# Converting float64 weights to float32: the rounding of the low word moved from VectorE to ScalarE and GpSimd

## The chip, the cores and the metric

One core of a Trainium2 chip runs the kernel. The metric is device time in microseconds of one execution, the median of several runs. VectorE, ScalarE, GpSimd, TensorE and SyncE are called DVE, ACT, POOL, PE and SP in rows of the profile.

## The reference

The kernel computes sliding-window attention with a linear bias for each head, and passes its output through two gated blocks:

```python
x = attn_out.transpose(0, 2, 1, 3).reshape(2304, 512)   # 4 batches, 8 heads of 64, 576 positions
x = ((x @ moe_w_a) * (x @ moe_w_b)) @ moe_w_out         # 512 -> 1536 -> 512
h = ((x @ moe2_w1) * (x @ moe2_w2)) @ moe2_w3           # 512 -> 1024 -> 1024
out = h @ moe2_w_out                                     # 1024 -> 512
```

q, k and v are float32. The seven weight matrices come as float64 and must be turned into float32 on the chip.

## The kernel before, in words

Each float32 product runs as three passes over a rounded high part and the rest: an operand is split into hi and lo, and lo*hi, hi*lo and hi*hi are summed in PSUM. The second block's w3 @ w_out is formed first and goes through DRAM (w34), so the second block has one product fewer for each token.

The work has three stages. First the attention: 16 units (a batch and two heads) of 5 query blocks each, 80 steps. Beside it a filler gives TensorE the first group's gated products, for tokens that are ready, once that group's six weight tiles are converted. Then the rest of group 0. Then groups 1 to 9: six of the first block, four of the second, each with two 128-column chunks, on tiles of 512 tokens. A chunk's product (`g1`) takes two PSUM accumulators; ScalarE copies one (L526), VectorE multiplies by the other (L528), ScalarE rounds the result to gh (L531), and GpSimd subtracts to get gl (L73). The second product reads gh and gl (L541, L559), and VectorE adds it to an accumulator in SBUF (L548, L566). After the attention eight PSUM tiles go round for all these products.

Weights are converted beside this. A weight tile is [128, 512] float64, loaded by SyncE's queue as pairs of 32-bit words (`raw`, 512 KB: one buffer during the attention, two after it). `convert` returns stages: s0 (ScalarE, L107) takes the absolute value of the high words as float32; s1 is five VectorE instructions: a compare and multiply that makes a mask (L113), the high word's bits shifted and masked (L117), its sign and top exponent bit put in (L120), the exponent alone as a power of two in `ce` (L123), and the low word times that power (L127); s3 (L132, GpSimd) adds the low word's part. Then `split` rounds to hi on ScalarE (L139) and subtracts on GpSimd (L73). The tile `ca` holds the value (two buffers, later three); `ce`, one buffer, holds the low word's part from L123 to L132. The copy of a w3 product on its way to DRAM (L441, L442) uses the same `ce` buffer.

`Stages` emits these stages in turns: a turn gives every part in work its next stage, fetches a load if a raw buffer is free, and starts one more part. A step of the attention pays 0.3 turns in the first batch and 0.6 after it; later each chunk of 512 tokens pays 512/400 turns. There are 76 conversions: 6 for group 0 beside the attention, 24 for w3 @ w_out, the others for groups 1 to 9. The order in which each engine's queue gets its instructions is settled by the framework's scheduler, which takes program order as priority and simulated times for readiness; a tile of a pool with one buffer waits until the last reader of the one before is done.

Of the kernel before, what the change touches and what calls it, by code (L numbers as in the profile page):

```python
# [19 lines left out]

# Float32 products run as three float32r passes: an operand x is the exact sum of
# hi = float32r(x) and lo = x - hi, and x*w = lo*hi' + hi*lo' + hi*hi' to float32's accuracy.
# The second block's w3 @ w_out is formed first: (g @ w3) @ w_out = g @ (w3 @ w_out).
# Weights come as float64: their words are put together as rounded float32 on the chip.

# [4 lines left out]

GROUPS = (6, 4)  # groups of two 128-column chunks of each block's inner features
TA, TN = 256, 512  # tokens of a tile: beside attention, and after it
HALF = 1280  # the token at which the accumulators are cut in two
LAG, NLAG = 8, 2  # steps of attention from the scores to the product with v, and to the norms
AT = (0, 0, 1, 3)  # steps of a unit at which the next one is transposed
V_AT = {2: 1, 6: 2}  # steps at which the second and the third unit's v are loaded
FILL = 0.75  # microseconds of the first group's products in a step of attention
PACE = (0.3, 0.6)  # turns of the weights' conversion in a step: the first batch, the others
TURN = 400  # tokens of a chunk for each turn later
WARM_UNITS, WARM = 3, 2  # L40
# [3 lines left out]
def attention_moe_moe(ctx, tc, q, k, v, w_a, w_b, w_o, w_1, w_2, w_3, w_o2, out):  # L44
# [24 lines left out]
    def f32(ap):  # L69
        return ap.bitcast(F32)  # L70
# [7 lines left out]

    # ---------------------------------------------------------------- weights
    def load_cols(w, c):  # L80
        """128 columns of a [512, .] weight: [128, 4 * 128] with the rows on 4 x 128 partitions."""
        raw = pools["conv"].tile([P, W, 2], I32, name="raw", bufs=pools["raws"])
        nc.sync.dma_start(
            out=raw.rearrange("p (k f) t -> p k (f t)", k=KC),
            in_=w[:, c * P:(c + 1) * P].bitcast(I32).rearrange("(k p) f -> p k f", p=P),
        )
        return raw

    def load_rows(w, r, c):
        """128 rows and 512 columns."""  # L90
        raw = pools["conv"].tile([P, W, 2], I32, name="raw", bufs=pools["raws"])
        nc.sync.dma_start(
            out=raw.rearrange("p f t -> p (f t)"),
            in_=w[r * P:(r + 1) * P, c * W:(c + 1) * W].bitcast(I32),
        )
        return raw

    def convert(raw, hi=None, lo=None, use=()):
        """Float64's two words as float32, to the nearest (0 below float32's exponents), and its
        split: stages, to be emitted one after the other, each when the one before has run."""  # L100
        hw, lw = raw[:, :, 1], raw[:, :, 0].bitcast(U32)
        a = pools["conv"].tile([P, W], F32, name="ca", bufs=pools["cas"])
        ai = a.bitcast(I32)
        es = []

        def s0():
            nc.scalar.activation(a, f32(hw), ACTF.Abs)  # L107

        def s1():
            e = pools["conv"].tile([P, W], F32, name="ce", bufs=1)  # L110
            ei = e.bitcast(I32)
            es.append(e)
            nc.vector.tensor_scalar(  # L113
                out=a, in0=a, scalar1=bits(0x38100000), scalar2=bits(0x3FFFFFF8),
                op0=ALU.is_ge, op1=ALU.mult,
            )
            nc.vector.scalar_tensor_tensor(  # L117
                out=ai, in0=hw, scalar=3, in1=ai, op0=ALU.logical_shift_left, op1=ALU.bitwise_and
            )
            nc.vector.scalar_tensor_tensor(  # L120
                out=ai, in0=hw, scalar=-(1 << 30), in1=ai, op0=ALU.bitwise_and, op1=ALU.bitwise_or
            )
            nc.vector.tensor_scalar(  # L123
                out=ei, in0=ai, scalar1=-(1 << 23), scalar2=None, op0=ALU.bitwise_and
            )

            nc.vector.scalar_tensor_tensor(  # L127
                out=e, in0=lw, scalar=2.0 ** -52, in1=e, op0=ALU.mult, op1=ALU.mult
            )

        def s3():
            nc.gpsimd.tensor_tensor(out=a, in0=a, in1=es[0], op=ALU.add)  # L132

        if hi is None:
            return [s0, s1, s3] + [lambda f=f: f(a) for f in use]
        return [s0, s1, s3, lambda: split(a, hi, lo)]
# [5 lines left out]
    class Stages:  # L142
        """Parts (load, stages of what it loads): a part's stages are emitted in turns one after
        the other, its load ahead of them; its second stage is the last to read the load."""

# [31 lines left out]

    # ---------------------------------------------------------------- attention
    conv_s = ExitStack()
# [15 lines left out]
    def consts():  # L195
# [4 lines left out]
        )  # L200
        # c - p - 128 for key column c of the window and query row p
        rel = raw_2.tile([P, 2 * P], F32, name="rel")
# [11 lines left out]
        )  # L214
        # the bias of each head, as the unscaled scores take it: a power of 2 times up to 8 bits
        for h in range(H):
            nc.gpsimd.tensor_scalar(
                out=relb[:, h, :], in0=rel, scalar1=slope[h] * float(D) ** 0.5, scalar2=None, op0=ALU.mult
            )
        # and for the two heads of a pair below each other  # L220
        for j in range(2):
# [13 lines left out]
    def load_unit(u, which=(0, 1, 2)):  # L235
        b, hp = units[u]
        for x in which:
# [7 lines left out]
            if x:  # L245
# [4 lines left out]
                continue  # L250
            # the last block of q has its two heads on the diagonal, zeros beside them
            for j in range(2):
                o = slice(j * D, (j + 1) * D)
                nc.sync.dma_start(out=t[o, NB - 1, o], in_=s[j, (NB - 1) * P:S, :])

    # q's blocks and k's side by side, as many of them at a time as a bank takes
    cols = [(x, i, (x * NB + i) * P) for x in range(2) for i in range(NB)]
# [3 lines left out]
    def prep(u):  # L261
        """Functions that transpose and split a unit's q, k and v: (tensor engine, others)."""

# [19 lines left out]
        def v_parts():  # L283
            # v's three bfloat16 parts: the upper half of v, of what is left of it, and of what is left then
            vr = v_raws[u % 3]
# [11 lines left out]
    def window(i):  # L297
        """Query rows, keys and key blocks of a query block; the groups of heads that it has side
        by side: the last block's rows are half as many, its two heads fill the partitions."""
        m = P if i < NB - 1 else LAST  # L300
        nb = 1 if i == 0 else 2
        return m, nb * P, nb, 2 if m == P else 1
# [33 lines left out]
    def keep_warm(cnt, x):  # L336
        """Matmuls for the tensor engine's clock alone, which falls when there is little work."""
        ps = mm_tile(W)
# [10 lines left out]
    def probs(u, i):  # L349
# [18 lines left out]
        )  # L368
        # keys, head, part, key block, query
        order = "p (a b c m) -> p a b c m" if nj == 2 else "p (b c a m) -> p a b c m"  # L370
# [36 lines left out]

    # ---------------------------------------------------------------- w3 @ w_out of the second block
    FB = DFF2 // P
# [7 lines left out]
    def w34_parts(pool, halves):  # L417
        """The product's two halves of the contraction, each its own array."""
        NJ = W // P
# [38 lines left out]

    # ---------------------------------------------------------------- gated blocks
    blocks = (dict(a=w_a, b=w_b, o=w_o), dict(a=w_1, b=w_2, o=w34))  # L460
    G1, NG = GROUPS[0], sum(GROUPS)
    # (block, its two chunks)
    groups = [(blk, (2 * g, 2 * g + 1)) for blk in range(2) for g in range(GROUPS[blk])]
# [3 lines left out]
    def weight_parts(g):  # L467
        """Loads of a group's weights and their splits, part by part."""
        blk, chunks = groups[g]
# [40 lines left out]
    def g1(g, n, t, tn):  # L510
        """A chunk's gated product for the tn tokens from t on."""
        assert whole[g] == 6
# [64 lines left out]
    def gate_items(gs, tiles, gap):  # L577
        """(function, cost, tokens that it needs) in the order of the tensor engine."""
        pend = []
        for g in gs:  # L580
            def first(g, n, t, tn):
                if g and t == tiles[1][0] and n == 0 and g + 1 < NG:
                    # the ring of the group before is free now
                    side.parts[0:0] = weight_parts(g + 1)
# [21 lines left out]

    # ---------------------------------------------------------------- the order of it all
    steps = [(u, i) for u in range(NU) for i in range(NB)]
    NS = len(steps)

    def attention_ops():
        """The functions of each step of attention, in order."""
        tops, late = [], []
# [37 lines left out]
    class Filler:  # L651
        """The first group's work, for when the tensor engine has nothing of attention's to do."""

# [100 lines left out]
```

## Time and profile before

| | |
|---|---|
| median of 3 runs | 1056.13 us |
| lowest, highest | 1048.25, 1060.08 us |
| span of the profiled execution | 1056.7 us |
| busy: TensorE, VectorE, GpSimd, ScalarE | 1017.9, 691.0, 494.3, 382.0 us |

The profile is of one execution. Its span runs from the first to the last instruction; no other time of that execution is given. Busy time of an engine includes what an instruction waits inside itself after its start.

### The profile page before, as it was taken

Reading aid. Unit: us, or ns where it says so; the run is one execution under the profiler, and the core shown is the slowest. Engines: PE = TensorE matmul, PEld = TensorE weight load, DVE = VectorE, ACT = ScalarE, POOL = GpSimd, SP = SyncE. Lnnn points to the kernel's source line nnn. Section 1 sums busy time; section 2 is a strip of 40 time slices with the busy share of each in tenths; the row PEclk is TensorE's granted clock in tenths of the full one; section 3 lists DMA queues with packets and bytes.
Section 4 is the critical chain, followed back from the end, with each engine's and each line's share of the span. In section 5 each row is a group of like instructions: output and inputs, shape, how many; then the busy total and the mean of one; then the engine's idle time right before and its main releaser. Section 6 shows DMA issues by size and latency. Waiting matters only on the chain.

```text
span 1056.7 us, 16482 instructions
## 1 busy us (share of the span) xinstructions
PE 1017.9 (96%) x6162; PEld 838.2 (79%) x6162; DVE 691.0 (65%) x1420; ACT 382.0 (36%) x929; POOL 494.3 (47%) x409
## 2 busy tenths in 40 slices
PE   7889999999999889999999999999999999999998
PEld 5567788787987778887788788888888888888886
DVE  6999997757499995587969659565273373322222
ACT  5555766655344232332333323233322221211110
POOL 6566645445267562264636226477572352421111
PEclk9688979878899899999999999999999999999999
DMA  6867676656333221232232223121021020000012
GB/s 140 170 122 154 118 114 121 123 101 115 81 100 100 79 100 70 74 107 73 99 109 84 77 71 99 60 80 41 1 80 40 20 81 20 20 1 1 11 70 100
DMA packets 160080, 85.23 MB, mean 81 GB/s; under 512 B 128000, under 2 KB 148992, under 8 KB 160000
## 3 DMA queue, kind: packets, MB, share of 16 engines
q1 hardware_dynamic: 160000, 84.18, 31.5%
q8 instruction: 48, 0.79, 0.3%
q14 instruction: 32, 0.26, 0.1%
HBM read 58.20 MB, written 8.91 MB: 64 GB/s over the span
## 4 chain that ended last, share of the span: by engine, by line
PE 62%; DVE 22%; DMA 6%; issue 6%; ACT 2%; POOL 1%; SPq 1%; DVEq 0%; ACTq 0%; POOLq 0%
PE mm L521 33%; PE mm L559 10%; PE mm L541 7%; DVE ca L117 4%; PE tr L388 4%; PE mm L439 4%; PE s L313 3%; DVE pe L357 3%; DVE ca L120 3%; DVE ca L113 2%; DVE ce L123 2%; DMA pt<-pp 2%; DVE ce L127 2%; DMA raw<-in_moe_w_out 1%; DVE pe L325 1%
## 5 line engine op out<-in xcount | busy, mean ns | idle before, releaser
L73 POOL TENSOR_TENSOR gl<-g,gh 128x512 fp32r<-128x512 f32 (+1 forms) x108 | 127.7, 1183 | 265.3 <-ACT gh L531 258.4
L132 POOL TENSOR_TENSOR ca<-ca,ce 128x512 f32<-128x512 f32 x76 | 104.7, 1378 | 138.2 <-DVE ce L127 127.4
L528 DVE TENSOR_TENSOR g<-a,mm 128x512 f32<-128x512 f32 (+1 forms) x108 | 64.1, 594 | 157.3 <-PE mm L521 146.7
L531 ACT ACTIVATE gh<-g 128x512 fp32r<-128x512 f32 (+1 forms) x108 | 60.4, 559 | 209.4 <-DVE g L528 209.1
L73 POOL TENSOR_TENSOR pp<-pe,pp 128x512 f16<-128x512 f32 (+1 forms) x80 | 81.8, 1030 | 73.1 <-ACT pp L363 39.9
L521 PE MATMUL mm<-x_hi,wlA 128*128 128x512 f32 (+1 forms) x464 | 109.2, 356 | 0.0
L521 PE MATMUL mm<-x_lo,whA 128*128 128x512 f32 (+1 forms) x464 | 106.9, 351 | 0.0
L521 PE MATMUL mm<-x_hi,whA 128*128 128x512 f32 (+1 forms) x464 | 106.2, 349 | 0.0
L521 PE MATMUL mm<-x_hi,wlB 128*128 128x512 f32 (+1 forms) x400 | 99.8, 371 | 5.5 <-DVE g L528 5.0
L526 ACT ACTIVATE a<-mm 128x512 f32<-128x512 f32 (+1 forms) x108 | 56.1, 519 | 126.6 <-PE mm L521 126.5
L521 PE MATMUL mm<-x_lo,whB 128*128 128x512 f32 (+1 forms) x400 | 98.8, 369 | 0.0
L521 PE MATMUL mm<-x_hi,whB 128*128 128x512 f32 (+1 forms) x400 | 98.7, 369 | 0.0
L521 PEld LDWEIGHTS mm<-x_lo,whA 128*128 128x128 f32 x464 | 80.3, 197 | 10.5
L521 PEld LDWEIGHTS mm<-x_hi,whA 128*128 128x128 f32 x464 | 79.7, 196 | 11.1
L113 DVE TENSOR_SCALAR ca<-ca 128x512 f32<-128x512 f32 x76 | 48.8, 642 | 60.4 <-ACT ca L107 60.4
L521 PEld LDWEIGHTS mm<-x_hi,wlA 128*128 128x128 f32 x464 | 78.6, 195 | 12.1 <-issue 0.6
L107 ACT ACTIVATE ca<-raw 128x512 f32<-128x512 f32 x76 | 50.9, 669 | 101.5 <-DMA raw<-in_moe_w 51.6
L521 PEld LDWEIGHTS mm<-x_hi,wlB 128*128 128x128 f32 x400 | 70.6, 188 | 19.9 <-DVE g L528 6.1
L117 DVE SCALAR_TENSOR_TENSOR ca<-raw,ca 128x512 int32<-128x512 int32 x76 | 82.4, 1084 | 1.6
L357 DVE TENSOR_SCALAR pe<-pe,st 128x256 f32<-128x256 f32 (+1 forms) x144 | 81.5, 602 | 1.3
L331 ACT ACTIVATE pe<-pe,st 128x256 f32<-128x256 f32 (+1 forms) x144 | 68.7, 478 | 37.6 <-DVE st L325 36.0
L120 DVE SCALAR_TENSOR_TENSOR ca<-raw,ca 128x512 int32<-128x512 int32 x76 | 80.9, 1065 | 1.5
(100 smaller groups left out, 2086.7 us busy)
## 6 DMA issues: line engine op xcount, KB each, us to landing
raw<-in_moe_w SPq DMA_DIRECT2D x32, 512.0 KB, 3.5
raw<-in_moe_w_out SPq DMA_DIRECT2D x20, 512.0 KB, 3.5
raw<-in_moe_w_a SPq DMA_DIRECT2D x12, 512.0 KB, 3.5
raw<-in_moe_w_b SPq DMA_DIRECT2D x12, 512.0 KB, 3.5
out<-acc SPq DMA_DIRECT2D x18, 256.0 KB, 2.0
q_raw<-in_q SPq DMA_DIRECT2D x32, 128.0 KB, 2.6
k_raw<-in_k SPq DMA_DIRECT2D x32, 128.0 KB, 2.8
v_raw<-in_v SPq DMA_DIRECT2D x32, 128.0 KB, 2.6
```

Of the source, the lines that this page charges most:

```text
L73: eng.tensor_tensor(out=out, in0=a, in1=b, op=ALU.subtract)
L113: nc.vector.tensor_scalar(out=a, in0=a, scalar1=bits(0x38100000), scalar2=bits(0x3FFFFFF8), op0=ALU.is_ge, op1=ALU.mult,)
L117: nc.vector.scalar_tensor_tensor(out=ai, in0=hw, scalar=3, in1=ai, op0=ALU.logical_shift_left, op1=ALU.bitwise_and)
L120: nc.vector.scalar_tensor_tensor(out=ai, in0=hw, scalar=-(1 << 30), in1=ai, op0=ALU.bitwise_and, op1=ALU.bitwise_or)
L132: nc.gpsimd.tensor_tensor(out=a, in0=a, in1=es[0], op=ALU.add)
L331: nc.scalar.activation(pe[:, j, :n], pe[:, j, :n], ACTF.Exp, bias=st[:, 0, j:j + 1], scale=-1.0, accum_out=st[:, 1, j:j + 1],)
L357: nc.vector.tensor_scalar(out=pe[:, j, :n], in0=pe[:, j, :n], scalar1=st[:, j:j + 1], scalar2=None, op0=ALU.mult)
L521: nc.tensor.matmul(p, w[:, z, kk, :], x[:, kk, o], start=(y == 0), stop=(y == len(terms) - 1))
L528: nc.vector.tensor_tensor(out=gg, in0=a, in1=ps[1], op=ALU.mult)
L531: nc.scalar.activation(gh, gg, ACTF.Copy)
L541: nc.tensor.matmul(p, w, x, start=(y == 0), stop=(y == len(terms) - 1))
L559: nc.tensor.matmul(p, x, w, start=(y == 0), stop=(y == len(terms) - 1))
```

## The change

s0 also rounds the low word, as an unsigned integer times 2^-29, to an integer number of units in the last place of the result, on ScalarE into `ce`. s1 becomes three VectorE instructions: a max that lifts small values, a shift and mask of the value's own bits, and the sign and top exponent bit from the high word. s3 adds the two as integers on GpSimd.

```diff
         def s0():
             nc.scalar.activation(a, f32(hw), ACTF.Abs)
+            e = pools["conv"].tile([P, W], I32, name="ce", bufs=1)
+            es.append(e)
+            nc.scalar.activation(e, lw, ACTF.Copy, scale=2.0 ** -29)
 
         def s1():
-            e = pools["conv"].tile([P, W], F32, name="ce", bufs=1)
-            ei = e.bitcast(I32)
-            es.append(e)
             nc.vector.tensor_scalar(
-                out=a, in0=a, scalar1=bits(0x38100000), scalar2=bits(0x3FFFFFF8),
-                op0=ALU.is_ge, op1=ALU.mult,
+                out=a, in0=a, scalar1=bits(0x38000000), scalar2=None, op0=ALU.max
             )
-            nc.vector.scalar_tensor_tensor(
-                out=ai, in0=hw, scalar=3, in1=ai, op0=ALU.logical_shift_left, op1=ALU.bitwise_and
+            nc.vector.tensor_scalar(
+                out=ai, in0=ai, scalar1=3, scalar2=0x3FFFFFF8,
+                op0=ALU.logical_shift_left, op1=ALU.bitwise_and,
             )
             nc.vector.scalar_tensor_tensor(
                 out=ai, in0=hw, scalar=-(1 << 30), in1=ai, op0=ALU.bitwise_and, op1=ALU.bitwise_or
             )
-            nc.vector.tensor_scalar(
-                out=ei, in0=ai, scalar1=-(1 << 23), scalar2=None, op0=ALU.bitwise_and
-            )
-            nc.vector.scalar_tensor_tensor(
-                out=e, in0=lw, scalar=2.0 ** -52, in1=e, op0=ALU.mult, op1=ALU.mult
-            )
 
         def s3():
-            nc.gpsimd.tensor_tensor(out=a, in0=a, in1=es[0], op=ALU.add)
+            nc.gpsimd.tensor_tensor(out=ai, in0=ai, in1=es[0], op=ALU.add)
```

## Rows read from the trace of the kernel before

**Rows 1.** Windows: start:end, length, busy us (instructions) of PE, PEld, DVE, ACT, POOL; PEclk; DMA; GB/s.
```profile
25.00:150.00 125.00, 113.47 (x1080) 86.92 (x1081) 118.48 (x375) 77.21 (x247) 74.00 (x67) 0.80 0.73 138
150.00:285.00 135.00, 131.71 (x1357) 108.87 (x1353) 91.18 (x347) 76.58 (x258) 61.99 (x62) 0.86 0.59 111
285.00:400.00 115.00, 103.88 (x558) 87.70 (x557) 107.80 (x134) 42.48 (x84) 71.40 (x50) 0.97 0.29 91
400.00:630.00 230.00, 226.16 (x1080) 187.37 (x1078) 160.63 (x232) 71.52 (x124) 97.26 (x71) 1.00 0.26 86
630.00:1050.00 420.00, 420.00 (x1991) 350.86 (x1990) 193.79 (x264) 100.54 (x180) 171.65 (x134) 1.00 0.13 44
```

**Rows 2.** The page's chain that ended last, by engine.
```profile
PE 62%; DVE 22%; DMA 6%; issue 6%; ACT 2%; POOL 1%; SPq 1%; DVEq 0%; ACTq 0%; POOLq 0%
```

**Rows 3.** Groups on DVE, 285 to 400 us: count, busy us, mean ns, idle before.
```profile
L117 DVE SCALAR_TENSOR_TENSOR ca<-raw,ca 128x512 int32<-128x512 int32 x21 | 27.2, 1297 | 0.4
L120 DVE SCALAR_TENSOR_TENSOR ca<-raw,ca 128x512 int32<-128x512 int32 x21 | 22.3, 1060 | 0.5
L127 DVE SCALAR_TENSOR_TENSOR ce<-raw,ce 128x512 f32<-128x512 uint32 x19 | 18.5, 972 | 0.5
L123 DVE TENSOR_SCALAR ce<-ca 128x512 int32<-128x512 int32 x19 | 16.1, 849 | 2.7 <-POOL ca L132 1.7
L113 DVE TENSOR_SCALAR ca<-ca 128x512 f32<-128x512 f32 x21 | 10.6, 504 | 4.2 <-ACT ca L107 4.2
```

**Rows 4.** Waits of PE, 285 to 400 us: total us, times, longest.
```profile
PE mm L521 <- DVE g L528: 5.0, 3, 2.5
PE mm L541 <- POOL gl L73: 4.1, 2, 2.4
```

**Rows 5.** Windows, the part of that stretch with a lower clock.
```profile
345.00:360.00 15.00, 11.51 (x45) 9.23 (x44) 14.07 (x19) 4.14 (x9) 8.65 (x7) 0.77 0.26 78
```

**Rows 6.** Timeline of DVE: start us, us, instruction.
```profile
316.92 0.41 DVE L113 TENSOR_SCALAR ca<-ca 128x512 f32<-128x512 f32 x1
317.36 1.66 DVE L117 SCALAR_TENSOR_TENSOR ca<-raw,ca 128x512 int32<-128x512 int32 x1
319.06 0.69 DVE L120 SCALAR_TENSOR_TENSOR ca<-raw,ca 128x512 int32<-128x512 int32 x1
```

**Rows 7.** Timeline of POOL about the same time.
```profile
310.92 1.28 POOL L73 TENSOR_TENSOR wlB<-ca,whB 128x512 fp32r<-128x512 f32 x1 [3.46 <-ACT whB L139]
...
317.07 1.40 POOL L132 TENSOR_TENSOR ca<-ca,ce 128x512 f32<-128x512 f32 x1 [0.63 <-DVE ce L127]
```

**Rows 8.** Groups on ACT, whole span.
```profile
L107 ACT ACTIVATE ca<-raw 128x512 f32<-128x512 f32 x76 | 50.9, 669 | 101.5 <-DMA raw<-in_moe_w 51.6 <-DMA raw<-in_moe_w_out 24.9 <-DMA raw<-in_moe_w_a 12.8
...
L139 ACT ACTIVATE whB<-ca 128x512 fp32r<-128x512 f32 x26 | 16.1, 628 | 34.7 <-POOL ca L132 30.5 <-PE mm L559 3.9
```

**Rows 9.** Groups on POOL, 285 to 400 us.
```profile
L132 POOL TENSOR_TENSOR ca<-ca,ce 128x512 f32<-128x512 f32 x19 | 28.2, 1483 | 18.2 <-DVE ce L127 18.2
...
L73 POOL TENSOR_TENSOR ol<-ca,oh 128x512 fp32r<-128x512 f32 x4 | 6.8, 1712 | 1.5 <-ACT oh L139 1.5
```

**Rows 10.** Waits of DVE, 400 to 630 us.
```profile
DVE ce L123 <- DMA w<-ce: 12.4, 10, 3.0
...
DVE ce L123 <- POOL ca L132: 4.6, 5, 1.4
```

**Rows 11.** Waits of SP's queue, 285 to 400 us.
```profile
SPq L92 <- DVE ce L127: 69.3, 13, 7.5
```

**Rows 12.** Windows of L132 alone (GpSimd's add, one for each conversion).
```profile
285.00:400.00 115.00, 28.18 (x19) 0.97 0.29 91
400.00:630.00 230.00, 40.84 (x30) 1.00 0.26 86
```

**Rows 13.** Groups on DVE, 25 to 110 us.
```profile
L117 DVE SCALAR_TENSOR_TENSOR ca<-raw,ca 128x512 int32<-128x512 int32 x6 | 6.6, 1100 | 0.0
...
L127 DVE SCALAR_TENSOR_TENSOR ce<-raw,ce 128x512 f32<-128x512 uint32 x6 | 4.5, 750 | 0.0
```

## The prediction

> **What bounds the kernel now.** I read the stages first, since a mean over the whole span hides them. The windows [rows 1] show five. In the attention, up to 150 us, VectorE is busy for 118.5 of 125 us while TensorE runs small matmuls with gaps; from 150 to 285 us VectorE falls to 91 of 135. From 285 to 400 us VectorE is busy for 107.8 of 115 us (94%) and TensorE is idle for 115 - 103.9 = 11.1 us. From 400 to 630 us TensorE is idle for 230 - 226.2 = 3.8 us. From 630 us on TensorE is busy in every microsecond at full clock, and what VectorE has to do there (194 of 420 us) is hidden. So a faster conversion can earn nothing after 630 us. The chain of waits agrees: 62% of it lies on TensorE and 22% on VectorE [rows 2].
>
> In the stretch from 285 to 400 us the largest VectorE groups are the five conversion lines [rows 3]: L117, L120, L127, L123 and L113, together 27.2 + 22.3 + 18.5 + 16.1 + 10.6 = 94.7 of the 107.8 us. TensorE waits there for L528 on VectorE (the gate product, queued behind conversions) and for the gl subtraction on GpSimd [rows 4]. And the clock is granted at only 0.77 between 345 and 360 us [rows 5], after such waits: 0.23 of 15 us, 3.4 us of full-rate work lost.
>
> The mean durations hide a second fact. One timeline [rows 6, 7]: L120 alone takes 0.69 us and L113 alone 0.41 us, but L117 at 317.36 takes 1.66 us. GpSimd's add began at 317.07 and took 1.40 us, to 318.47; L117 ended at 319.02, 0.55 us later. So L117 got almost nowhere while GpSimd ran. The two engines largely exclude each other on these SBUF-to-SBUF instructions, and the resource is the pair. Its load between 285 and 400 us, with about 20 conversions (21 of L117, 19 of L127 [rows 3]): VectorE alone 2 x 0.41 + 3 x 0.69 = 2.9 us each, so 58 us; GpSimd 71.4 us [rows 1], of which perhaps 64 without its own waits (50 instructions there, nearly all of 1.28 us [rows 7] or shorter). Together 122 us in 115: this pair is the bound.
>
> **The change part by part.** *VectorE.* Five instructions become three. The compare and multiply (L113) becomes a max of the same form, L120 stays, and L117 and L123 give way to one shift-and-mask with one tensor input, which is L123's own form (int32, scalars, SBUF to SBUF). L127 goes. So one form like L117 and one like L127 are removed: 1.297 + 0.972 = 2.27 us a conversion between 285 and 400 us at the measured means, 2 x 0.69 = 1.38 us uncontended [rows 3, 6]. An integer pair of operations on one tensor input does stand in the trace (L123), so the new forms are bounded: 0.41 us alone, 0.85 mean.
>
> *ScalarE* gets one Copy from 8-byte-strided words to integers. The trace has the same read with a float output, L107 at 669 ns, and a contiguous one, L139 at 628 ns [rows 8]. No row shows uint32 in and int32 out; I bound it between these two, a little below (a function's cost might not depend on type) and twice L107 above, and take 0.67. ScalarE is busy for 42.5 of 115 us [rows 1]; 20 x 0.67 = 13 us makes 56. In the attention six of them add 4 us to 77 of 125.
>
> A rule of the Trainium skill speaks against this: the page "ScalarE: Activation LUTs", section "Rules for kernel authors", says to multiply on VectorE and not on ScalarE, since VectorE is up to about three times as fast for each element. By the rule the product would be dearer where it goes. The rows do not bear that out: L127, which held it, takes 0.97 us here [rows 3], L107 takes 0.67 [rows 8]. The rule's factor would make the ScalarE instruction some 2.1 us (estimate: 3 x 0.69), 29 us more over 20 conversions on an engine with 72 us idle there, and the sum would stand.
>
> *GpSimd.* The add becomes an integer add. No integer row exists on GpSimd. The nearest row is the same add in float32, 1.48 us in this stretch; the dearest 512-wide row is 1.71 us [rows 9]. Below, it could be as short as 0.6 us, were half the work conversion; above, I allow double, 2.96 us. I take 1.48, being the same width, the same two inputs and the same bytes.
>
> *The pair after.* VectorE alone 2 x 0.41 + 0.69 = 1.51 us, 30 us for 20 conversions; with GpSimd's 64 it is 94 us in the same 115. Where the load was 106% it is 82%.
>
> *Waits.* The ce tile has one buffer. VectorE used to take it at L123, midway; now ScalarE takes it at the start of the conversion, and so waits for the GpSimd add of the conversion before, and in the stage of the w3 product for the DMA of a product's result, which uses the same buffer. VectorE waited 12.4 us for that DMA and 4.6 us for that add from 400 to 630 us, 15 times [rows 10]. These waits move into ScalarE's queue, ahead of the evacuation L526, of gh L531 and of the splits L139. I cost them at nothing, since PSUM holds eight accumulators of which each takes TensorE several microseconds: if that cover is gone, 17 us of waits have somewhere to land. The raw buffer is freed by whichever comes last of the third VectorE instruction and ScalarE's rounding. Today the load waits for L127, 69.3 us over 13 loads [rows 11], and L127 itself stands behind L123, which needs the add before. The new order puts one ScalarE instruction of 0.67 us between that add and the release, in place of L123 and L127 (0.85 + 0.97), so SyncE's queue moves a little sooner.
>
> *Sum.* From 285 to 400 us TensorE can win back 11.1 us idle and the 3.4 us of clock, 14.5. Since the pair drops below full but not to little, I take three quarters: 11. From 400 to 630 us, 30 conversions [rows 12] and 3.8 us idle: 2.5, since part of it waits for the w3 split and not for conversions. In the attention the six conversions lie between 25 and 110 us, where VectorE is nearly always busy: 6.6 + 4.5 = 11.1 us leave it [rows 13], 4 us come onto ScalarE, which is in the same chain of exponentials; between 0 and 11 I take 5. Together 18.5 us. The profiled execution spans 1056.7 us; no other time of it is known, and it lies 0.6 us above the median of the runs, 1056.1, so the sum holds for either: 1038 us.
>
> **The rivals.**
> *B, the pair stays the bound.* If GpSimd always goes first, VectorE's three instructions are still held for a GpSimd instruction each, TensorE's waits for gl [rows 4] stay, and the attention gains nothing because its VectorE work waits for GpSimd and for ScalarE. For it: 1.66 against 0.69 in the timeline. Against: the pair's load falls by 28 us. One third of 18.3 us (14.5 + 3.8) is won: 1051 us. The page "Advanced Engine Details and Errata" of the Trainium skill, section "VectorE Performance Modes", gives the mechanism: VectorE's second SBUF port is shared with GpSimd and the two block each other. By that rule the two new single-input instructions, which it would count among those that use both ports, stay exposed; L113 at 0.50 mean against 0.41 alone agrees mildly, L123 at 0.85 strongly.
>
> *C, slower: ScalarE stops in its queue for ce.* Place: the rounding of a conversion, waiting for the add before it or for the DMA of a w3 product, with L526 and L531 of the gate behind it. For it: one buffer, held from ScalarE's rounding until GpSimd's add, now over the three VectorE instructions too, and shared with 16 product copies. Against: TensorE has a reserve of eight accumulators. Price: there are about 50 conversions between 285 and 630 us; each 0.1 us of stall that reaches TensorE costs 5 us. From 18.5 / 50 = 0.37 us a conversion on, the change loses. At 0.6 us it is 30 us lost against 18.5 won: 1068 us.
>
> *D, the work is only moved.* The integer add is twice as long: 1.48 x 20 = 30 us more on the pair, which gives back all of its 28. Only the attention gains 2 us: 1055 us.
>
> **How the numbers follow.** Forecast 0.60 (its own range 1026 to 1046), B 0.20, C 0.12, D 0.08. A measurement of this kernel, whose three runs spread from 1048 to 1060, tells about 1%, 10.6 us, from no change: faster is under 1045.6 and slower over 1066.7. Nearly all of the forecast and a little of B lie below the first: 0.62. Two thirds of C lie above the second, and a reordered attention can add a little: 0.10. The rest, 0.28, is within. The range: everything won, 18.3 and 11.1, is 1027, and 7 us more for a clock that stays up in the attention gives 1020; upwards, B, D and the mild half of C reach 1060.
>
> **What would show it.** Right: three VectorE lines for each conversion, 2.4 to 2.7 us in sum between attention and 400 us; VectorE there at 60 to 70% in place of 94%; TensorE idle there under 4 us and no fall of the clock; the attention's end some 5 us earlier; the last stage as long as before. Wrong: ScalarE's rounding with idle time released by GpSimd's add or by the DMA of ce, over 20 us in total, and TensorE waiting for gh or gl behind it (C); VectorE's shift-and-mask at over 1 us mean (B); the integer add far from 1.4 us (D).

## The result, and the profile after

The changed kernel takes 1024.0 us (median of 4 runs, 1019.6 to 1029.6), beside 1056.6 us for the kernel before. The ratio is 0.9735, with a 95% interval from 0.969 to 0.978: faster by 2.65%, 28 us of 1056. The forecast was 1038 us in a range from 1020 to 1060. The two medians alone would give 0.969, the lower edge of the interval: these runs of the kernel before took longer than its later ones beside the experiments, with medians of 1052.4 to 1054.2 us. Effects are given as ratios below, each to the runs of before on the same chip. The profiled execution after spans 1025.0 us, before 1056.7; that one too is some 4 us long, so differences between the two traces are a little too large. One run of 1045.1 us, of the kernel with the slower pace below, fell in a slower state and is not counted.

The windows of the changed kernel (columns as in [rows 1]):

```profile
25.00:150.00 125.00, 115.01 (x1123) 88.42 (x1123) 110.58 (x385) 82.84 (x266) 75.33 (x70) 0.84 0.77 141
150.00:285.00 135.00, 129.22 (x1430) 109.25 (x1429) 101.09 (x341) 82.61 (x266) 68.00 (x68) 0.96 0.59 120
285.00:400.00 115.00, 111.49 (x555) 93.51 (x556) 73.00 (x95) 51.44 (x97) 63.83 (x48) 1.00 0.30 94
400.00:630.00 230.00, 230.00 (x1129) 192.90 (x1128) 128.02 (x192) 95.83 (x168) 108.35 (x84) 1.00 0.30 95
```

Between 285 and 400 us VectorE is busy for 73.0 of 115 us, 63%, where it was 94%. TensorE is idle for 3.5 us and not 11.1, at full clock throughout (0.97 before), and from 400 to 630 us it is busy all the time. The chain of waits, on the page, has moved from VectorE (22% in [rows 2]) to TensorE:

```profile
PE 77%; DVE 8%; DMA 5%; issue 3%; ACT 3%; POOL 3%; SPq 1%; POOLq 0%; DVEq 0%; ACTq 0%
```

The three VectorE groups of the conversion in that stretch, which answer to the five of [rows 3]:

```profile
L122 DVE SCALAR_TENSOR_TENSOR ca<-raw,ca 128x512 int32<-128x512 int32 x19 | 21.8, 1149 | 0.4
L118 DVE TENSOR_SCALAR ca<-ca 128x512 int32<-128x512 int32 x19 | 19.6, 1032 | 0.5
...
L115 DVE TENSOR_SCALAR ca<-ca 128x512 f32<-128x512 f32 x18 | 11.0, 613 | 6.6 <-ACT ca L108 6.4
```

In sum 2.79 us a conversion, from 4.68. What TensorE still waits for between 285 and 630 us comes to 4.1 us (before it waited 5.0 and 4.1 us for two of these lines alone [rows 4]):

```profile
PE mm L536 <- POOL gl L73: 1.3, 2, 1.1
PE mm L536 <- ACT gh L526: 1.2, 1, 1.2
PE mm L516 <- ACT acc L541: 1.2, 1, 1.2
PE mm L516 <- DVE g L523: 0.4, 1, 0.4
```

The other half of the gain lies earlier. SyncE's timeline tells where the attention ends, by the first weight load of group 1, which needs the attention's memory. Before:

```profile
281.29 0.39 SPq L83 DMA_DIRECT2D raw<-in_moe_w_a  x1
```

And after:

```profile
265.88 0.40 SPq L83 DMA_DIRECT2D raw<-in_moe_w_a  x1
```

So of the 31.7 us between the two spans, 15.4 lie before the end of the attention and 16.3 behind it. The attention's progress can be counted by its 80 reciprocals, one in each step (windows of that one VectorE line; the x column is the count, then the clock). Before:

```profile
40.00:100.00 60.00, 2.32 (x15) 0.80 0.68 143
```

After:

```profile
40.00:100.00 60.00, 2.80 (x18) 0.83 0.81 150
```

Eighteen steps in 60 us in place of 15, while the six conversions of group 0 run. Three steps at the slower rate are 3 x 60/15 = 12 us.

The moved work, over the whole span, in ScalarE's groups:

```profile
L111 ACT ACTIVATE ce<-raw 128x512 int32<-128x512 uint32 x76 | 50.8, 669 | 64.3 <-POOL ca L127 27.2 <-DMA w<-ce 25.0 <-DMA raw<-in_moe_w 11.9
L108 ACT ACTIVATE ca<-raw 128x512 f32<-128x512 f32 x76 | 50.6, 666 | 71.4 <-DMA raw<-in_moe_w 39.6 <-DMA raw<-in_moe_w_a 13.6 <-DMA raw<-in_moe_w_out 7.7
```

and in GpSimd's:

```profile
L127 POOL TENSOR_TENSOR ca<-ca,ce 128x512 int32<-128x512 int32 x76 | 100.4, 1322 | 137.4 <-ACT ce L111 74.1 <-DVE ca L122 32.9 <-issue 10.5
```

The rounding takes what the read of the high word takes, 669 and 666 ns, though its types differ. The integer add is no dearer than the float add: 1322 ns over the span, where the float add took 1378, and between 285 and 400 us 1357 ns, where it took 1483 [rows 9]. And the rounding does wait for ce as rival C said: 27.2 us for the add before and 25.0 us for the DMA of a product.

### The profile page after: what moved, and what is told of

It reads as the page before. It is cut to its first block, busy times and chain, and to the rows that moved or that the text cites. A ratio compares the mean times of both kernels' runs of the same rounds, so it can differ in the third digit from the quotient of the medians.

```text
span 1025.0 us, 16425 instructions
## 1 busy us (share of the span) xinstructions
PE 995.2 (97%) x6162; PEld 822.8 (80%) x6162; DVE 561.5 (55%) x1268; ACT 424.2 (41%) x1005; POOL 476.3 (46%) x409
## 4 chain that ended last, share of the span: by engine, by line
PE 77%; DVE 8%; DMA 5%; issue 3%; ACT 3%; POOL 3%; SPq 1%; POOLq 0%; DVEq 0%; ACTq 0%
PE mm L516 43%; PE mm L536 13%; PE mm L554 10%; PE mm L434 4%; PE tr L383 3%; DVE pe L352 3%; DMA pt<-pp 3%; PE s L308 2%; DVE pe L320 1%; DMA raw<-in_moe_w_a 1%; DMA raw<-in_moe_w_b 1%; PE tr L269 1%; DVE st L339 1%; ACT pe L326 1%; PE mm L426 1%
## 5 line engine op out<-in xcount | busy, mean ns | idle before, releaser
L73 POOL TENSOR_TENSOR gl<-g,gh 128x512 fp32r<-128x512 f32 (+1 forms) x108 | 124.7, 1154 | 279.1 <-ACT gh L526 278.9
L127 POOL TENSOR_TENSOR ca<-ca,ce 128x512 int32<-128x512 int32 x76 | 100.4, 1322 | 137.4 <-ACT ce L111 74.1
L73 POOL TENSOR_TENSOR pp<-pe,pp 128x512 f16<-128x512 f32 (+1 forms) x80 | 79.4, 999 | 59.3 <-ACT pp L358 36.1
L115 DVE TENSOR_SCALAR ca<-ca 128x512 f32<-128x512 f32 x76 | 44.6, 587 | 86.8 <-ACT ca L108 86.4
L122 DVE SCALAR_TENSOR_TENSOR ca<-raw,ca 128x512 int32<-128x512 int32 x76 | 81.9, 1078 | 1.8
L543 DVE TENSOR_TENSOR acc<-acc,mm 128x512 f32<-128x512 f32 (+1 forms) x100 | 62.0, 629 | 37.2 <-PE mm L536 36.9
L516 PEld LDWEIGHTS mm<-x_lo,whB 128*128 128x128 f32 x400 | 71.1, 188 | 12.8
L516 PEld LDWEIGHTS mm<-x_hi,whB 128*128 128x128 f32 x400 | 71.0, 189 | 12.5
```

The source lines that it names most:

```text
L73: eng.tensor_tensor(out=out, in0=a, in1=b, op=ALU.subtract)
L115: nc.vector.tensor_scalar(out=a, in0=a, scalar1=bits(0x38000000), scalar2=None, op0=ALU.max)
L122: nc.vector.scalar_tensor_tensor(out=ai, in0=hw, scalar=-(1 << 30), in1=ai, op0=ALU.bitwise_and, op1=ALU.bitwise_or)
L127: nc.gpsimd.tensor_tensor(out=ai, in0=ai, in1=es[0], op=ALU.add)
L516: nc.tensor.matmul(p, w[:, z, kk, :], x[:, kk, o], start=(y == 0), stop=(y == len(terms) - 1))
L543: nc.vector.tensor_tensor(out=ya, in0=ya, in1=p, op=ALU.add)
```

## The experiments

Nine kernels were run, each beside the kernel before on the same chip. The edits are shown against the changed kernel, cut to the lines that matter.

### Where the gain lies: the two halves alone

The new conversion for group 0 alone. Here `convert_new` is the changed kernel's conversion and `convert` the old one; their definitions are left out:

```diff
-                return convert(raw, hi, lo) + [count]
+                return (convert_new if g == 0 else convert)(raw, hi, lo) + [count]
```

> The three-instruction conversion for the six weight tiles of group 0 alone (those beside the attention), the old one for the other 70. If the attention's gain is VectorE time taken out of a stretch that VectorE bounds, the last reciprocal of the attention moves from 268.7 us to about 257 us, as in the changed kernel, and the whole time is about 1056.6 - 12 = 1045 us (1040 to 1049). If the attention's gain came from a different order of the queues, or from luck with the clock, its end lies anywhere between 250 and 275 us, and the time with it.

Measured: 1040.1 us, ratio 0.9891 (0.9852 to 0.9930), as the first reading had it; the last reciprocal comes at 252.9 us, even earlier than the 257 expected. Steps between 40 and 100 us:

```profile
40.00:100.00 60.00, 2.94 (x19) 0.86 0.80 152
```

The other half, the old conversion (here `convert_old`) for group 0 and the new one (`convert`) everywhere else:

```diff
-                return convert(raw, hi, lo) + [count]
+                return (convert_old if g == 0 else convert)(raw, hi, lo) + [count]
```

> The other half: the old conversion for group 0, the new one for the other 70. VectorE theory: the attention ends as before (268 us), TensorE's idle time between the attention and 630 us still falls to about 4 us, and the time is about 1024 + 12 = 1036 us (1032 to 1042). Rival (the attention's gain is a matter of order): the time is under 1030 or over 1045, with the attention's end to account for it.

Measured: 1034.9 us, ratio 0.9845 (0.9809 to 0.9882). Steps:

```profile
40.00:100.00 60.00, 2.31 (x15) 0.73 0.71 144
```

and the stretch behind the attention:

```profile
285.00:400.00 115.00, 111.11 (x578) 94.16 (x577) 76.30 (x96) 53.03 (x102) 67.39 (x52) 1.00 0.29 95
```

The halves add up: 1.09% and 1.55%, together 2.64%, and the change has 2.65%. In microseconds of 1056 they are 11.5 (7.4 to 15.6) in the attention and 16.4 (12.5 to 20.2) behind it. The first batch's pace follows the group 0 conversions alone: 18 or 19 steps with the new one, 15 with the old one, whatever the rest of the kernel does. That the attention's gain was a matter of another queue order is out for this part: four queue orders, two rates, and the rate goes with the conversion. Only the end of the attention in the second kernel is not as expected: its last reciprocal came at 261.8 us, not at 268, after a like 98.9 us at the 26th (99.6 before). In the execution profiled of before TensorE ran at half clock (0.50 granted) from 202 to 222 us, and steps 61 to 66 took 21 us there against 13 to 17 in all other traces; I put some 5 of the 15.4 us between the two profiles down to that execution and not to the change (an estimate from these steps).

### Is it VectorE's time?

The last VectorE instruction of each conversion, which gives the same bits when repeated, issued three times, so that VectorE has five instructions again:

```diff
+            for _ in range(3):
                 nc.vector.scalar_tensor_tensor(
                     out=ai, in0=hw, scalar=-(1 << 30), in1=ai, op0=ALU.bitwise_and, op1=ALU.bitwise_or
                 )
```

> The changed kernel with its last VectorE instruction of each conversion issued three times (the same bits each time), so that VectorE has five instructions again, three of the dearer form, 2.9 us alone; the rounding stays on ScalarE and the integer add on GpSimd. VectorE theory: the gain goes, 1050 to 1062 us, the attention ends near 268 us again and VectorE is over 90% busy in the 115 us behind it. Rival (the gain is the shorter chain from the add to the free raw buffer, or the moved place of ce): most of the gain stays, 1024 to 1035 us.

Measured: 1049.6 us (median of 10), ratio 0.9961 (0.9930 to 0.9993), a hair under the 1050 to 1062 of the VectorE reading; the attention's last reciprocal comes at 272.8 us (268.7 before). The profile is of the longest of the ten runs (1057.1 us), so it shows the loss a little too large. The steps are back, and so is the stretch:

```profile
40.00:100.00 60.00, 2.12 (x15) 0.80 0.70 140
```
```profile
285.00:400.00 115.00, 103.98 (x558) 87.98 (x557) 107.31 (x132) 52.95 (x103) 67.61 (x50) 0.96 0.29 94
```

VectorE 107.3, TensorE idle for 11.0 us, clock 0.96: the stretch of the kernel before (107.8, 11.1, 0.97 [rows 1]), with the rounding still on ScalarE and the add still in integers. So 2.26 of the 2.65 points go with VectorE's instructions, and not with the place of the rounding, the integer add or ce. The other 0.4 points (4 us, with an interval from 0.1 to 0.7 points) no run explains. The repeats also make each conversion some 1.4 us longer, so a rival is that TensorE waits for weights that come later. The trace speaks against it: no weight is among TensorE's waits in that stretch, and the largest is for the gate product on VectorE, as before (5.0 us [rows 4]):

```profile
PE mm L517 <- DVE g L524: 6.3, 3, 3.4
```

The cheap form instead, the max issued three times: 2 x 0.41 us alone and not 2 x 0.69.

```diff
+            for _ in range(3):
                 nc.vector.tensor_scalar(
                     out=a, in0=a, scalar1=bits(0x38000000), scalar2=None, op0=ALU.max
                 )
```

> The changed kernel with the max of each conversion issued three times (the same bits), so VectorE has five instructions again, but the two more are the cheap form: 2 x 0.41 us alone, 2.3 us for a conversion in place of 1.5 (before: 2.9; sign three times: 2.9). If the time follows VectorE's load, it loses 0.82 / 1.38 = 0.6 of what the sign issued three times lost (25 us): about 1039 us. If it is a matter of VectorE being full or not between the attention and 400 us, only the attention loses (6 x 0.82 = 5 us): 1026 to 1032 us.

Measured: 1036.6 us, ratio 0.9845 (0.9785 to 0.9906): 1.1 points lost against 2.26, a half, where the load alone says 0.6. With the two intervals the loss is 0.35 to 1.85 points, so the time alone does not exclude that only the attention loses (5 us, 0.5 points). The trace does: behind the attention TensorE is idle for 8.8 us (3.5 in the change) with VectorE at 83%:

```profile
285.00:400.00 115.00, 106.24 (x521) 87.86 (x520) 95.48 (x132) 50.53 (x93) 62.77 (x48) 0.99 0.28 92
```

Its largest wait there is again for the gate product, and VectorE's timeline shows the longest of the three. TensorE stands for 3.8 us, until 332.0, while VectorE works through a whole conversion ahead of the gate product (L524):

```profile
PE mm L517 <- DVE g L524: 5.5, 3, 3.8
```
```profile
325.95 3.28 DVE L116 TENSOR_SCALAR ca<-ca 128x512 f32<-128x512 f32 x3
329.27 1.38 DVE L119 TENSOR_SCALAR ca<-ca 128x512 int32<-128x512 int32 x1
330.68 0.69 DVE L123 SCALAR_TENSOR_TENSOR ca<-raw,ca 128x512 int32<-128x512 int32 x1
331.29 0.68 DVE L524 TENSOR_TENSOR g<-a,mm 128x512 f32<-128x512 f32 x1
```

So VectorE needs room, not just less than 100%.

### Rival C: ScalarE's queue

ScalarE's rounding issued twice:

```diff
+            for _ in range(2):
                 nc.scalar.activation(e, lw, ACTF.Copy, scale=2.0 ** -29)
```

> The changed kernel with ScalarE's rounding issued twice, 76 x 0.67 = 51 us more on ScalarE and the ce buffer held 0.67 us longer. Forecast's theory (ScalarE's work is hidden, its waits for ce too): at most 4 us in the attention and nothing behind it, 1024 to 1029 us. Rival C (ScalarE's queue is near the path): each of some 50 conversions before 630 us costs 0.3 us or more, 1039 us or above.

Measured: 1023.8 us, ratio 0.9733 (0.9692 to 0.9774), not to be told from the change. ScalarE's groups show 50.6 us more on it:

```profile
L112 ACT ACTIVATE ce<-raw 128x512 int32<-128x512 uint32 x152 | 101.4, 667 | 62.2 <-POOL ca L128 27.1 <-DMA w<-ce 22.3 <-DMA raw<-in_moe_w 11.8
```

Behind the attention they cost nothing: TensorE is busy there all the time, from 285 to 630 us:

```profile
285.00:400.00 115.00, 115.00 (x602) 98.36 (x602) 77.60 (x102) 65.81 (x123) 67.85 (x52) 1.00 0.32 103
```

In the attention the trace does show something. Steps between 40 and 100 us, 18 in the change:

```profile
40.00:100.00 60.00, 2.65 (x17) 0.77 0.77 144
```

The 26th reciprocal comes at 91.1 us and the last at 261.9. In the three traces that have the new conversion there with one rounding and the same pace (the change, the kernel with the new conversion in group 0 alone, and the next one below) they come at 86.5 to 89.6 and at 252.9 to 259.3 us. So with 4 us more on ScalarE the attention is 1.5 to 4.6 us later at the 26th step, in one execution; the whole time, known to 0.4%, cannot show whether that is lost.

The other test puts the copy of the w3 product in a buffer of ca, so that the rounding no longer waits for its DMA:

```diff
-                sb = pools["conv"].tile([P, DM], F32, name="ce", bufs=1)
+                sb = pools["conv"].tile([P, DM], F32, name="ca", bufs=pools["cas"])
```

> The changed kernel with the copy of the w3 product in a buffer of ca (three of them) and not in the one of ce. Forecast's theory (ScalarE's waits for ce are covered): ScalarE's 25 us of waits for the product's DMA go, and the time stays within 4 us, 1020 to 1028 us. Rival C in part (these waits reach TensorE): 5 us or more are won, 1019 us or below.

Measured: 1021.7 us, ratio 0.9725 (0.9687 to 0.9762), not to be told from the change. The rounding's waits for ce are nearly as long as before, now for the add alone (49.4 us, where the change has 27.2 for the add and 25.0 for the DMA):

```profile
ACT ce L111 <- POOL ca L127: 49.4, 34, 4.4
```

Rival C falls by the first test, as it was priced: 51 us more in ScalarE's queue do not show in the time, and in the change TensorE waits only 3.7 us behind the attention for ScalarE's gh and acc and for GpSimd's gl, in the rows above. The second test cannot show what less waiting would be worth, since that kernel has hardly less of it. A second buffer of ce for every conversion was not tried.

### Rival B: the pair of VectorE and GpSimd

The subtraction of each split issued twice on GpSimd:

```diff
+        for _ in range(2):
             sub(nc.gpsimd, lo, f, f32(hi))
```

> The changed kernel with GpSimd's subtraction of each conversion's split issued twice (the same bits), 1.3 us more for each conversion on GpSimd and nothing on VectorE. If VectorE and GpSimd exclude each other, the pair's load between the attention and 400 us rises by some 20 x 1.28 = 26 us to about 120 of 115 and TensorE waits again: 1034 us or above, with longer VectorE instructions (shift and mask over 1.1 us, sign over 1.3). If VectorE's own time was the bound and the pair does not matter, GpSimd has the room (64 to 90 of 115 us): 1024 to 1029 us.

Measured: 1041.2 us, ratio 0.9901 (0.9877 to 0.9925): 1.66 points, 17 us, lost by GpSimd work alone. Steps and stretch:

```profile
40.00:100.00 60.00, 2.53 (x16) 0.75 0.77 147
```
```profile
285.00:400.00 115.00, 108.56 (x558) 91.25 (x558) 81.20 (x95) 52.09 (x101) 88.90 (x66) 0.97 0.29 96
```

VectorE has the same instructions as in the change and is busy for 81.2 us in place of 73.0; its three groups rise from 2.79 to 3.21 us:

```profile
L122 DVE SCALAR_TENSOR_TENSOR ca<-raw,ca 128x512 int32<-128x512 int32 x20 | 24.8, 1242 | 0.6
L118 DVE TENSOR_SCALAR ca<-ca 128x512 int32<-128x512 int32 x20 | 21.7, 1083 | 0.6
L115 DVE TENSOR_SCALAR ca<-ca 128x512 f32<-128x512 f32 x20 | 17.6, 882 | 20.3 <-ACT ca L108 20.3
```

So GpSimd's time is VectorE's time in part. The time came out as the exclusion said; the two limits on single instructions were not passed (shift-and-mask 1.08 us, sign 1.24), and L115 took most of the rise. Of the 14.4 us between the profiled spans (1039.4 and 1025.0), 8.6 lie before the end of the attention, by the first load of group 1 (274.52 and 265.88 us), and 5.8 behind it. How much of either is the exclusion, and how much GpSimd's own queue (its subtraction for the probabilities is a link of the attention's chain), stays open.

### The pace of the conversions

Whether the freed time can be spent otherwise was tried with two other paces of the first batch, the rest as in the change:

```diff
-PACE = (0.3, 0.6)
+PACE = (0.4, 0.6)
```

> The changed kernel with 0.4 turns of conversion in a step of the first batch in place of 0.3, so that group 0 is converted some 15 us earlier and the filler can start then. If VectorE's freed time in the attention can carry this, TensorE fills more of the attention: 1014 to 1022 us. If VectorE bounds the first batch as before, the steps there only get slower and nothing is won: 1022 to 1030 us.

Measured: 1030.5 us, ratio 0.9780 (0.9744 to 0.9816).

```diff
-PACE = (0.3, 0.6)
+PACE = (0.22, 0.6)
```

> The changed kernel with 0.22 turns of conversion in a step of the first batch in place of 0.3. The six conversions spread over more steps, and the filler starts some 20 us later. If the first batch's steps are bounded by what the conversions put on VectorE at each step, they run faster, and at most the filler's delay is lost: 1018 to 1026 us. If what counts is how early the filler can start, 1028 to 1036 us.

Measured: 1031.4 us (median of three runs), ratio 0.9773 (0.9721 to 0.9826). Neither can be told from the change, whose interval (0.969 to 0.978) overlaps both; both ratios are some 0.4 points worse. The steps, first with the faster and then with the slower pace:

```profile
40.00:100.00 60.00, 2.54 (x16) 0.76 0.71 141
40.00:100.00 60.00, 2.96 (x19) 0.85 0.78 153
```

With more conversion in each step the steps get slower, as they do where VectorE bounds them (16 in 60 us, 18 in the change); with less they hardly get faster (19). No version that was run beats the change beyond its interval.

## Why the prediction was right, point by point

**The time.** The change won 28 us where the sum had 18.5, and 1024.0 us lies below the forecast's own range (1026 to 1046). It is inside the outer range because that left room for everything won (1027) and for 7 us of clock in the attention. No row gave that 7. The granted clock from 150 to 285 us did go from 0.86 to 0.96, but it is 0.94 also in the kernel that keeps the old conversion in the attention, so I do not count it as the change's.

**What bounds the kernel.** Right for VectorE behind the attention, and shown by the VectorE instructions put back: the same rows return with them. That the pair of VectorE and GpSimd is the bound was too simple. By the prediction's own count the pair is full again in the kernel with GpSimd's subtraction issued twice (94 + 18 x 1.28 = 117 of 115 us), yet TensorE idles for 6.4 us there and not 11: here a microsecond on GpSimd costs less than one on VectorE, which also has the gate product to do.

**VectorE, five to three.** The count and forms were right. The durations were 2.79 us a conversion, a little over the 2.4 to 2.7 that I gave, because the shift-and-mask took 1.03 us in place of L123's 0.85 [rows 3]: alone both take some 0.43 us, but 10 of its 19 instructions took 1.37 to 1.42, held up beside GpSimd as below; of L123's 19, five took 1.33 or more.

**ScalarE and GpSimd.** Both values held: 669 ns for the rounding (0.67 taken) and 1.36 us in the same stretch for the integer add (1.48 taken). The rule of the Trainium skill, in "ScalarE: Activation LUTs", section "Rules for kernel authors", prefers VectorE for a multiply, but the prediction read it too widely: that page of the Trainium skill gives its factor of about three for bf16 and a single source. Here the words have 32 bits and VectorE's multiply had two tensor inputs, so 3 x 0.69 was no fair estimate. The measurement decides: 13 of 19 of VectorE's multiplies (L127 between 285 and 400 us) took 0.68 or 0.69 us (0.97 in the mean, with the time beside GpSimd), where ScalarE's takes 0.67, and ScalarE had the time to give.

**Behind the attention.** 13.5 us forecast (11 and 2.5), 16.4 (12.5 to 20.2) by the kernel that changes only this part. The mechanism was right in its place, its idle time (3.5 us, under 4 as I asked) and its clock. I gave back a quarter for a pair that stays near full; the two stages together won most of 18.3.

**The attention.** This is the term that was mis-sized: "between 0 and 11 I take 5", and it is 11.5 (7.4 to 15.6). The step that failed is the halving, for the 4 us that come onto ScalarE in the same chain of exponentials. The change has these 4 us, and still the VectorE time taken out of the stretch came back: 11.1 us [rows 13], 11.5 measured. Why they did not count is not shown. The kernel that rounds twice does not settle it, since its attention came out later by about what it added.

**Rival B** is half true. Its sign came: the shift-and-mask at over 1 us in the mean (1.03). The exclusion is there, as a VectorE line of the change beside a GpSimd line shows. VectorE's timeline:

```profile
305.52 1.40 DVE L118 TENSOR_SCALAR ca<-ca 128x512 int32<-128x512 int32 x1
306.96 0.69 DVE L122 SCALAR_TENSOR_TENSOR ca<-raw,ca 128x512 int32<-128x512 int32 x1
```

and GpSimd's:

```profile
305.23 1.41 POOL L127 TENSOR_TENSOR ca<-ca,ce 128x512 int32<-128x512 int32 x1 [0.63 <-DVE ca L122]
```

L118, 0.43 us for its form alone, takes 1.40 and ends 0.28 us after the add, which ends at 306.64. The note of "Advanced Engine Details and Errata" in the Trainium skill, section "VectorE Performance Modes", that VectorE's second port is shared with GpSimd, and that GpSimd and VectorE's two-port instructions block each other, agrees with this. What does not hold is B's condition that GpSimd always goes first: in the rows of before, L113 had begun when GpSimd's add began, and took its 0.41 us [rows 6], while the add took 1.40 where GpSimd's subtraction took 1.28 [rows 7]. In these rows the one that starts first runs on. And the price of B was wrong: with 1.28 us of each conversion still lost this way (2.79 against 1.51 alone), TensorE had its work.

**Rival C** had half of its sign (52 us of waits of the rounding for ce, but only 2.5 us of TensorE's for gh and gl) and not its price. **Rival D** did not happen: the add is not dearer.

## What to carry to other kernels

In a stretch that one engine bounds, time taken from that engine can come back whole, as it did here, so do not halve it for a price on another engine that no row shows. Put the load back with a repeated, harmless instruction, and the rows say whether that engine's time was the bound. Look at VectorE and GpSimd together when both work on SBUF: the mean duration of a VectorE line then contains GpSimd's time. And a long list of waits on an engine off the path, 52 us here, says nothing until one has looked at whether TensorE's waits changed with it.

## What was not expected of the hardware

An instruction on ScalarE that reads uint32 with an 8-byte stride and writes int32 takes 669 ns, the same to 3 ns as one that reads and writes float32, and 76 more of them did not move the whole time (1023.8 against 1024.0 us). GpSimd's add of two int32 tiles takes 1.32 us in the mean where the float32 add took 1.38 over the span, and the medians are the same (1.294 and 1.297 us); no penalty for integers shows.
